# A fused attention kernel: score matmuls over 32 rows in four row groups, a corrected scheduling table and a third buffer set

## The chip, the cores and the metric

The kernel runs on one core of one Trainium2 chip. The metric is device time in microseconds (us), the median of several executions; less is better. In the profile, PE is the matmul engine, PEld its weight loads, ACT the engine that computes exponentials (ScalarE), DVE the vector engine. The granted clock is the share of its full speed that PE's throttle allowed. PSUM is the memory that matmuls write. All runs quoted are fast unless the text says otherwise.

## The reference, cut to what matters

Four blocks on `x` of 2048 tokens and 512 features: multi-query softmax attention (32 heads of 16, one K and one V for all heads), a linear-attention block, and the same two again.

```python
q = (x @ wq).reshape(B, S, 32, 16) ...     # 32 heads
k = x @ wk; v = x @ wv                     # one head of 16 for all
scores = einsum("bhqd,bkd->bhqk", q, k) * 16 ** -0.5
o = einsum("bhqk,bkd->bhqd", softmax(scores), v) ...   # then @ wo
# block B: phi(q) (phi(k)^T v) / den, then @ wo          (linear attention)
```

The two softmax blocks have 2 * 32 * 2048 * 2048 scores. The kernel cuts them into 4096 tiles of 128x512.

## The kernel before: the parts that matter

**Scores.** A head has only 16 features. Q of eight heads lies in 128 partitions, and K is stored in masked copies: in copy `m`, each group of `RG` partitions keeps only the rows of its m-th head, the others are zero. A score matmul contracts one group of `RG` rows against one copy. With `RG = 64` there are two row groups and four copies. Matmuls in different row groups can run at the same time (the timelines below show it).

```python
RG = 64
NRG, NM = P // RG, RG // DH            # 2 row groups, 4 masked copies
i, m = j % NRG, b * (4 // NRG) + j // NRG
r = slice(i * RG, (i + 1) * RG)
x = e.matmul(bank(b0 + k), lhsT=Kr[r, m, kt*P:(kt+1)*P],
             rhs=QT[r, ...], start=True, stop=True)
```

**Two ways to an exponential.** PSUM has eight banks of 128x512. Banks 0 to 2 and 3 to 5 are two *sets*: PE fills one set with three score tiles while ACT turns the other into bf16 exponentials with one instruction (128x1536, "wide"). In parallel, single tiles go through bank 6 to DVE, which approximates the exponential in seven steps, the first on each tile, the other six on pairs of tiles. Bank 7 accumulates the product with V. Whatever else needs a bank (projections, transposes) takes bank 6, or borrows bank 5 (`SHARE`); while that one is lent, ACT gets two tiles only (128x1024, "narrow").

**The order is made at build time.** A small list scheduler simulates the engines with a table of durations and writes a fixed order for each engine. No engine chooses another order at run time:

```python
def tdv(n, c=1.04): return 0.065 + n * c * 1e-3      # DVE, us
def tac(n):         return 0.09 + n * 0.833e-3       # ACT, us
o = add(PE, 0.05 + 0.14 * m, f, ..., name="sA")      # a set of m scores
```

**The filler.** So that PE's clock stays up, the scheduler adds dummy matmuls (zero weights, 512 columns, into the accumulator) wherever PE is idle in its plan and the array streamed less than 0.6 of the last 1.7 us:

```python
st = {"pv": 0.071, "sA": 0.4, "dummy": 0.2}.get(o.name, 0.85 * o.dur[PE])
...                                   # summed over the last 1.7 us
if streaming(now) > FILL * FILLW: return      # FILL, FILLW = 0.6, 1.7
o = add(PE, ..., lambda e: e.matmul(bank(7, FILLN), lhsT=zer[:], ...), name="dummy")
```

The softmax here doesn't subtract the row's maximum and nothing guards it: scores larger than these inputs give would overflow.

## Time and profile before

Median 1849.07 us (1846.9 to 1851.51, 3 runs).

From the page of the kernel before: the span, busy time by engine, the granted clock in 40 slices (9 is 90% or more), and the chain of work that ended last, by engine and by line.

```profile
span 1845.4 us, 26741 instructions
...
PE 1754.5 (95%) x11002; PEld 515.1 (28%) x11002; DVE 1658.7 (90%) x2966; ACT 1739.9 (94%) x1529; POOL 34.2 (2%) x46
...
PEclk9999999999999999999999999999999999999999
...
PE 44%; DVE 43%; ACT 11%; issue 1%; POOL 1%; DMA 0%; SPq 0%
PE ps_all L635 17%; PE ps_all L671 13%; ACT PTA L775 10%; DVE xT L829 9%; DVE PTD L851 8%; PE ps_all L496 7%; DVE xs L850 5%; DVE xs L847 5%; DVE xu L846 4%; DVE xu L849 3%; DVE xs L848 2%; PE ps_all L897 2%; PE ps_all L692 1%; DVE Eo L683 1%; DVE stats L461 1%
...
```

All three engines look nearly full, and the chain changes engine all the time. Neither says what a faster PE is worth. The groups of instructions by shape say more (count, busy us, mean ns of one, then the idle time before them and what ended it):

```profile
...
L775 ACT ACTIVATE PTA<-ps_all 128x1536 bf16<-128x1536 f32 x1039 | 1437.1, 1478 | 57.6 <-PE ps_all L635 50.7
L635 PE MATMUL ps_all<-QT,Kr 64*128 64x512 bf16 x4096 | 835.1, 383 | 42.0 <-DVE xT L829 16.0 <-ACT PTA L775 13.3 <-DVE Osb L701 1.1
...
L829 DVE TENSOR_SCALAR xT<-ps_all 128x512 int32<-128x512 f32 x523 | 358.8, 686 | 48.9 <-PE ps_all L635 45.7
...
L775 ACT ACTIVATE PTA<-ps_all 128x1024 bf16<-128x1024 f32 x227 | 235.5, 1038 | 1.7 <-PE ps_all L635 1.4
L897 PE MATMUL ps_all<-maskx,zer 128*128 128x512 bf16 x594 | 205.0, 387 | 0.0
...
L511 DVE TENSOR_SCALAR Kr<-ps_all,mpar 128x256 bf16<-128x256 f32 x45 | 21.5, 480 | 3.2 <-PE ps_all L496 1.5 <-ACT Kr L510 1.4
...
L510 ACT ACTIVATE Kr<-ps_all,mpar 128x256 bf16<-128x256 f32 x19 | 9.0, 473 | 2.1 <-DVE Kr L511 1.5
...
```

L775 are the exponentials on ACT, wide and narrow; L635 the score matmuls; L829 the first DVE step of a score tile, so 523 of 4096 tiles go to DVE; L897 the dummies; L511 and L510 the evictions of K into its masked copies, 45 + 19 = 64.

A shown duration contains waiting and overlap with the next instruction. The interval from one start to the next is a better price. Where ACT is saturated, a wide exponential starts 1.330 us after the one before it and a narrow one takes 0.903 us. I use that for a balance: **ACT's need** is, for each shape, its count times the 10th percentile of its start-to-start interval; **lateness** is how much longer the intervals after exponentials are in all. For the kernel before, the need is 1698 us, the lateness 47 us after wide and 61 us after narrow exponentials, and 39 us of the span of 1845 us remain (layer starts and ends, mostly).

The timeline of PE (start, length, instruction, how many in a row):

```profile
...
500.62 0.39 PE L635 MATMUL ps_all<-QT,Kr 64*128 64x512 bf16 x2
...
1099.92 0.60 PE L635 MATMUL ps_all<-QT,Kr 64*128 64x512 bf16 x3
...
1104.42 0.82 PE L635 MATMUL ps_all<-QT,Kr 64*128 64x512 bf16 x4
...
```

Two score matmuls in different row groups take as long as one; each time that a row group is needed again, another 0.21 us is added (0.60 and 0.82 us). Who waited for score matmuls (total us, times, longest):

```profile
...
ACT PTA L775 <- PE ps_all L635: 52.1, 127, 1.5
DVE xT L829 <- PE ps_all L635: 45.7, 88, 1.5
...
```

### The profile page before, as it was taken

How to read it: one execution, taken by the hardware profiler on the slowest of the kernel's cores; microseconds unless marked ns; L12 is line 12 of the kernel's file. 1: busy time of each engine (PE TensorE's matmuls, PEld its weight loads, DVE VectorE, ACT ScalarE, POOL GpSimd, SP SyncE). 2: the span in 40 equal slices, each digit the busy share in tenths (PEclk: the TensorE clock that was granted, in tenths of full speed). 3: DMA queues.
4: the chain of work that ended last, by engine and by line, in shares of the span. 5: the costliest groups of instructions: out<-in, count | busy, mean ns of one | idle time of the engine just before them, and what ended most of it. 6: DMA issues, size and time to landing. Idle time of an engine off the chain costs nothing.

```text
span 1845.4 us, 26741 instructions
## 1 busy us (share of the span) xinstructions
PE 1754.5 (95%) x11002; PEld 515.1 (28%) x11002; DVE 1658.7 (90%) x2966; ACT 1739.9 (94%) x1529; POOL 34.2 (2%) x46
## 2 busy tenths in 40 slices
PE   7999999999999999999899999999999999999998
PEld 3222222222222222223342222222223222232224
DVE  7999988999889997998689999899997999989985
ACT  7999999999999999999699999999999999999996
POOL 0000000000000000000000000000000000000000
PEclk9999999999999999999999999999999999999999
DMA  3000000000000000000000000000000000000001
GB/s 115 1 1 1 1 1 1 1 1 1 1 1 1 1 1 1 1 1 1 1 1 1 1 1 1 1 1 1 1 1 1 1 1 1 1 1 1 1 1 46
DMA packets 7722, 9.08 MB, mean 5 GB/s; under 512 B 1456, under 2 KB 7088, under 8 KB 7600
## 3 DMA queue, kind: packets, MB, share of 16 engines
q1 hardware_dynamic: 7600, 7.37, 1.2%
q8 instruction: 86, 1.41, 0.3%
q14 instruction: 36, 0.29, 0.1%
HBM read 5.28 MB, written 2.10 MB: 4 GB/s over the span
## 4 chain that ended last, share of the span: by engine, by line
PE 44%; DVE 43%; ACT 11%; issue 1%; POOL 1%; DMA 0%; SPq 0%
PE ps_all L635 17%; PE ps_all L671 13%; ACT PTA L775 10%; DVE xT L829 9%; DVE PTD L851 8%; PE ps_all L496 7%; DVE xs L850 5%; DVE xs L847 5%; DVE xu L846 4%; DVE xu L849 3%; DVE xs L848 2%; PE ps_all L897 2%; PE ps_all L692 1%; DVE Eo L683 1%; DVE stats L461 1%
## 5 line engine op out<-in xcount | busy, mean ns | idle before, releaser
L775 ACT ACTIVATE PTA<-ps_all 128x1536 bf16<-128x1536 f32 (+1 forms) x1268 | 1640.6, 1398 | 59.4 <-PE ps_all L635 52.1
L635 PE MATMUL ps_all<-QT,Kr 64*128 64x512 bf16 x4096 | 835.1, 383 | 42.0 <-DVE xT L829 16.0
L671 PE MATMUL ps_all<-PTA,Vaug 128*32 128x512 bf16 x3573 | 539.3, 389 | 3.4 <-DVE Eo L683 2.8
L829 DVE TENSOR_SCALAR xT<-ps_all 128x512 int32<-128x512 f32 x523 | 358.8, 686 | 48.9 <-PE ps_all L635 45.7
L851 DVE SCALAR_TENSOR_TENSOR PTD<-xT,xs 128x1024 uint16<-128x1024 int32 (+1 forms) x262 | 318.4, 1215 | 1.4
L635 PEld LDWEIGHTS ps_all<-QT,Kr 64*128 64x128 bf16 x4096 | 175.2, 93 | 500.9 <-ACT PTA L775 198.2
L671 PEld LDWEIGHTS ps_all<-PTA,Vaug 128*32 128x32 bf16 x3573 | 129.5, 93 | 463.4 <-issue 451.5
L897 PE MATMUL ps_all<-maskx,zer 128*128 128x512 bf16 x594 | 205.0, 387 | 0.0
L846 DVE TENSOR_SCALAR xu<-xT 128x1024 f16<-128x1024 uint16 (+1 forms) x262 | 180.2, 688 | 3.0
L850 DVE TENSOR_TENSOR xs<-xs,xu 128x1024 f16<-128x1024 f16 (+1 forms) x262 | 179.0, 684 | 3.0
L847 DVE TENSOR_TENSOR xs<-xu 128x1024 f16<-128x1024 f16 (+1 forms) x262 | 178.7, 682 | 2.0
L671 PE MATMUL ps_all<-PTD,Vaug 128*32 128x512 bf16 x523 | 144.3, 385 | 16.4 <-DVE Eo L683 12.9
L848 DVE TENSOR_SCALAR xs<-xs 128x1024 f16<-128x1024 f16 (+1 forms) x262 | 109.6, 418 | 2.1
L849 DVE TENSOR_SCALAR xu<-xu 128x1024 f16<-128x1024 f16 (+1 forms) x262 | 109.5, 418 | 0.0
L897 PEld LDWEIGHTS ps_all<-maskx,zer 128*128 128x128 bf16 x594 | 48.7, 96 | 105.0 <-issue 98.3
L496 PE MATMUL ps_all<-wqkv_sb,xnT 128*128 128x512 bf16 x256 | 70.9, 383 | 3.3 <-DVE xnT L485 1.1
L469 POOL TENSOR_TENSOR rstd<-veps,mhalf 128x1 f32<-128x1 f32 x30 | 30.7, 1025 | 1731.1 <-DVE veps L467 1723.3
L940 DVE TENSOR_SCALAR e_buf<-e_buf 128x512 f32<-128x512 f32 x64 | 26.9, 422 | 32.8 <-ACT e_buf L939 32.5
L671 PEld LDWEIGHTS ps_all<-PTD,Vaug 128*32 128x32 bf16 x523 | 32.3, 94 | 65.3 <-DVE Eo L683 27.7
L692 PE MATMUL ps_all<-identf,Eo 128*128 128x128 f32 x256 | 42.0, 287 | 5.6 <-DVE Eo L683 4.0
L939 ACT ACTIVATE e_buf<-ps_all 128x512 f32<-128x512 f32 x64 | 39.0, 610 | 8.3 <-PE ps_all L496 6.1
L461 DVE BATCH_NORM_STATS2 stats<-x_sb 128x6 f32<-128x512 bf16 x64 | 43.2, 683 | 3.3 <-DMA x_sb<-in_A_x_dram 2.6
(87 smaller groups left out, 841.6 us busy)
## 6 DMA issues: line engine op xcount, KB each, us to landing
out_dram<-x_sb SPq DMA_DIRECT2D x16, 128.0 KB, 1.7
x_sb<-in_A_x_dram SPq DMA_DIRECT2D x3, 512.0 KB, 6.7
wqkv_sb<-in_B_wqkv_dram SPq DMA_DIRECT2D x1, 1536.0 KB, 11.6
x_sb<-in_A_x_dram SPq DMA_DIRECT2D x2, 256.0 KB, 3.1
wq_sb<-in_A_wq_dram SPq DMA_DIRECT2D x1, 512.0 KB, 4.6
wo_sb<-in_A_wo_dram SPq DMA_DIRECT2D x1, 512.0 KB, 8.5
wo_sb<-in_B_wo_dram SPq DMA_DIRECT2D x1, 512.0 KB, 10.9
wk_sb<-in_A_wk_dram SPq DMA_DIRECT2D x1, 16.0 KB, 2.6
```

What stands on the lines that cost most here:

```text
L496: i = e.matmul(bank(h.idx, n), lhsT=l, rhs=r, start=(c + k == 0), stop=(c + k == len(mms) - 1))
L635: x = e.matmul(bank(b0 + k), lhsT=Kr[r, m, kt * P:(kt + 1) * P], rhs=QT[r, self.units[u][0] % 2, gs, q0:q0 + n], start=True, stop=True)
L671: return e.matmul(ps[32 * c:32 * c + 32, 7 * 512:8 * 512], lhsT=Vaug[:, kt, :], rhs=src, start=opened[0], stop=opened[1], skip_group_check ...
L775: oe = add(AC, tac(m * 512), lambda e: e.activation(PTA[:, hp.idx, 0:m * 512], bank(3 * s, m * 512), ACTF.Exp, scale=SCALE), deps=[o] + pr ...
L829: o = add(DV, tdv(512), lambda e: e.tensor_scalar(out=xT[:, hx.idx, i * 512:(i + 1) * 512], in0=bank(6), scalar1=SCALE * LOG2E * 65536.0, ...
L846: o = add(DV, tdv(w, 0.52), lambda e: e.tensor_scalar(out=u_, in0=lo, scalar1=1.0 / 65536, scalar2=-0.5, op0=ALU.mult, op1=ALU.add), deps= ...
L847: o1 = add(DV, tdv(w, 0.52), lambda e: e.tensor_tensor(out=s_, in0=u_, in1=u_, op=ALU.mult), deps=[o] + c["prev"], name="xsq", **kw)
L848: o2 = add(DV, tdv(w, 0.26), lambda e: e.tensor_scalar(out=s_, in0=s_, scalar1=XK, scalar2=-XW, op0=ALU.mult, op1=ALU.add), deps=[o1], nam ...
L849: o3 = add(DV, tdv(w, 0.26), lambda e: e.tensor_scalar(out=u_, in0=u_, scalar1=1.0, scalar2=XL, op0=ALU.mult, op1=ALU.add), deps=[o1], nam ...
L850: o4 = add(DV, tdv(w, 0.52), lambda e: e.tensor_tensor(out=s_, in0=s_, in1=u_, op=ALU.mult), deps=[o2, o3], name="xc", **kw)
L851: o5 = add(DV, tdv(w), lambda e: e.scalar_tensor_tensor(out=PTD[:, hp.idx, 0:w].bitcast(U16), in0=xT[:, k, 0:w], scalar=2.0 ** -9, in1=s_, ...
L897: o = add(PE, 0.03 + FILLN * 0.41e-3, lambda e: e.matmul(bank(7, FILLN), lhsT=zer[:], rhs=maskx[:].bitcast(BF16)[:, 0:FILLN], start=not ow ...
```

## The change

Scores are to contract 32 rows, so that a set of three uses three of four row groups at once. Two masked copies of K instead of four halve the evictions of K and free the memory for a third set of DVE buffers. The scheduler's table is corrected.

```diff
-    RG = 64
+    RG = 32                      # 4 row groups, 2 masked copies of K
-    NPA, NPD, NDX = 5, 6, 2
+    NPA, NPD, NDX = 5, 6, 3      # sets of DVE buffers
     def tdv(n, c=1.04):
-        return 0.065 + n * c * 1e-3
+        return 0.068 + n * c * 1e-3
     def tac(n):
-        return 0.09 + n * 0.833e-3
+        return 0.0525 + n * 0.8325e-3
... (seven smaller entries, nearly all DVE's: 0.18 -> 0.09, 0.14 -> 0.062, 0.4 -> 0.333 ...)
-            o = add(PE, 0.05 + 0.14 * m, f, ..., name="sA")
+            o = add(PE, 0.2 + 0.014 * m if RG == 32 else 0.05 + 0.14 * m, f, ..., name="sA")
-            st = {"pv": 0.071, "sA": 0.4, "dummy": 0.2}.get(...)
+            st = {"pv": 0.071, "sA": 0.2 if RG == 32 else 0.4, "dummy": 0.2}.get(...)
```

More of the change, by code (lines that the diff above doesn't have):

```diff
@@ L461, in layer_norm @@
         add(DV, tdv(512), lambda e: e.bn_stats(stats[:, t, 0:6], x_sb[:, t, :]), reads=[("x", t)], writes=[("st", t)], prio=prio, name="bn")
-        add(DV, 0.18, lambda e: e.bn_aggr(mv[:, t, :], stats[:, t, 0:6]), reads=[("st", t)], writes=[("mv", t)], prio=prio - 0.01)
+        add(DV, 0.09, lambda e: e.bn_aggr(mv[:, t, :], stats[:, t, 0:6]), reads=[("st", t)], writes=[("mv", t)], prio=prio - 0.01)
         if ctl.ramp or ctl.tail:
@@ L466, in layer_norm @@
         else:
-            add(DV, 0.14, lambda e: e.tensor_scalar(out=veps[:, t:t + 1], in0=mv[:, t, 1:2], scalar1=1e-5, scalar2=None, op0=ALU.add),
+            add(DV, 0.062, lambda e: e.tensor_scalar(out=veps[:, t:t + 1], in0=mv[:, t, 1:2], scalar1=1e-5, scalar2=None, op0=ALU.add),
                 reads=[("mv", t)], writes=[("ve", t)], prio=prio - 0.02)
@@ L485, in cp @@
             return f(xnT[:, :, t * P:(t + 1) * P], bank_bf(hb.idx))
-        o2 = add((DV, AC), {DV: 0.4, AC: tac(512)}, cp, deps=[o], uses=[hb], rel=[hb] + ([win] if win else []), writes=[("xnT", t)], prio=prio - 0.04, name="xnT", cb=cb)
+        o2 = add((DV, AC), {DV: 0.333, AC: tac(512)}, cp, deps=[o], uses=[hb], rel=[hb] + ([win] if win else []), writes=[("xnT", t)], prio=prio - 0.04, name="xnT", cb=cb)
     def proj(h, mms, n, reads, prio, chunk=2, name="proj"):
@@ L513, in k_proj @@
                 ops = {}
-            ops[m] = add((DV, AC), {DV: tdv(b - a), AC: tac(b - a)}, ev, deps=[o] + ([ops[m - 1]] if m else []), uses=[h], rel=[h] if m == NM - 1 else [],
+            ops[m] = add((DV, AC), {DV: 0.06 + tdv(b - a), AC: 0.1 + tac(b - a)}, ev, deps=[o] + ([ops[m - 1]] if m else []), uses=[h], rel=[h] if m == NM - 1 else [],
                          reads=["mpar"], writes=[("K", m, t) for t in range(t0, t0 + n)], prio=prio - 0.05, name="kev")
@@ L694, in norm @@
             o = add(PE, 1.0, tr, reads=["identf"], deps=[oe], acq=[ht, hos] if par == 0 else [ht], uses=[he], rel=[he], prio=1.2, name="trA")
-            o = add(DV, 0.246, lambda e: e.reciprocal(rden[:, hr.idx, :].unsqueeze(2), bank(ht.idx).rearrange("p (a c) -> p a c", c=32)[:, :, DH:DH + 1]),
+            o = add(DV, 0.168, lambda e: e.reciprocal(rden[:, hr.idx, :].unsqueeze(2), bank(ht.idx).rearrange("p (a c) -> p a c", c=32)[:, :, DH:DH + 1]),
                     deps=[o], acq=[hr], uses=[ht], prio=0.0, name="recA")
@@ L769, in f @@
                 return self.smm(e, got, 3 * s)
-            o = add(PE, 0.05 + 0.14 * m, f, reads=self.keys(got), deps=prev, uses=[h], prio=0.0, name="sA")
+            o = add(PE, 0.2 + 0.014 * m if RG == 32 else 0.05 + 0.14 * m, f, reads=self.keys(got), deps=prev, uses=[h], prio=0.0, name="sA")
             hp = Holder(p_pta)
@@ L881, in streaming @@
                 break
-            st = {"pv": 0.071, "sA": 0.4, "dummy": 0.2}.get(o.name, 0.85 * o.dur[PE])
+            st = {"pv": 0.071, "sA": 0.2 if RG == 32 else 0.4, "dummy": 0.2}.get(o.name, 0.85 * o.dur[PE])
             end = o.t0 + o.dur[PE]
@@ L921, in cp @@
             return fn(OT[:, :, g, :] if fine else OT[:, g, :, :], bank_bf(h.idx))
-        o2 = add((DV, AC), {DV: 0.4, AC: tac(512)}, cp, deps=[o], uses=[h], rel=[h], writes=keys, prio=pr, name="otc")
+        o2 = add((DV, AC), {DV: 0.333, AC: tac(512)}, cp, deps=[o], uses=[h], rel=[h], writes=keys, prio=pr, name="otc")
         if fine:
@@ L1021, in kv_block @@
                 for g in (2 * hh, 2 * hh + 1):
-                    add(DV, tdv(P, 0.52), lambda e, g=g: e.tensor_scalar(out=zb[:, g, :], in0=maskx[:, 0:P], scalar1=zf[:, g:g + 1], scalar2=None, op0=ALU.mult),
+                    add(DV, 0.195, lambda e, g=g: e.tensor_scalar(out=zb[:, g, :], in0=maskx[:, 0:P], scalar1=zf[:, g:g + 1], scalar2=None, op0=ALU.mult),
                         reads=[("zf", hh), "mask"], writes=[("zb", g)], prio=0.75, name="zb")
```

## The prediction

> **What bounds the kernel now.** No engine is full, but ScalarE's exponentials set the pace. The busy table gives PE 95%, ACT 94%, DVE 90% of 1845 us. PE's figure is not load (modelled ends, pipelined). ACT's contains hidden waiting: a saturated 128x1536 exponential starts 1.33 us after the one before it (median, timeline), yet is shown 1.48 us long. By such starts, 1039 wide (1.33) and 227 narrow (128x1024, 0.90) exponentials need 1382 + 205 us, and all of ACT about 1690. So some 155 us of ACT are lost: 105 us idle (52 us for score matmuls, waits view), the rest inside durations. The narrow ones, where the third bank is lent, start 1.17 us apart in the mean and lose about 60 us; the wide ones about 47. DVE (523 score tiles) needs about 1600 us and waits 46 us for score matmuls.
>
> **What the change does.**
> - Scores. In the timeline two score matmuls take 0.39 us, three 0.60, four 0.82: a set of three needs two array passes. With four row groups three start together: 0.40 us. That frees about 0.21 us for 1039 sets, 220 us of PE. The Trainium skill ("TensorE: Matmul & The Clock Gate", Part 3) gives 3.07x for four 32-row tiles; this trace shows two 64-row tiles overlapping, not yet four.
> - During a narrow exponential (0.90 us) PE must refill the other set: about 0.4 us of signalling and order plus 0.60 of matmuls does not fit; with 0.40 it just does. I expect 35 of the 60 us back, and 15 of the 47.
> - K: 64 evictions become 32; DVE loses about 10 us of work, ACT 4.5 us, at layer starts; perhaps 6 us of span.
> - Scheduling table: it decides a static order. The old one charged 1.369 us for a wide exponential, the new one 1.331, what the trace shows. The old one paced ACT 3% too slow and gave DVE too many tiles; perhaps 10 us. A third DVE buffer set covers some of DVE's waits.
> - Against it: the filler that keeps the clock up sees half the streaming per set and adds dummies (0.22 us each); from 594 I expect about 1300. They eat much of the freed PE time, but enter only where the schedule has PE idle. Narrow exponentials stay near 230.
>
> "TensorEngine Tiling (Array Packing)", PSUM Bottleneck, says that tiling speeds up TensorE but not PSUM evacuation; that is why only waiting, not ACT or DVE work, is won here: about a quarter of the 220 us.
>
> **Sum.** 35 + 15 + 6 + 10, less some lost to dummies and to DVE not keeping up: about 50 us. Predicted 1798 us, 8 in 10 between 1755 and 1838. Faster by over 2% (below 1812): 0.64; within 2%: 0.32; slower: 0.04.
>
> **What would show it.** Three score matmuls in 0.40 us; narrow exponentials about 1.0 us apart in the mean; ACT's waits for scores below 30 us; ACT busy about 96%; dummies over 1000; 32 K evictions; granted clock 1.00 throughout; DVE tiles 500 to 540.
>
> **What would make it wrong.** Row groups that don't run together; the filler delaying score sets as before; a lower clock; the lent bank, not matmul time, stalling narrow sets (then about 1835); ACT waiting for the order of PE's queue behind DVE-released work, which faster scores don't cure; DVE taking over as the limit. If the corrected table matters more than I think, below 1760.

## The result and the profile after

Median 1799.83 us (1795.13 to 1806.72, 4 runs) against 1849.94 us (4 runs) before: ratio 0.9734, 95% interval 0.9692 to 0.9776. All ratios here are the mean time of one kernel's fast runs over that of the other's fast runs of the same rounds, so not quite the ratio of the medians.

The same parts of the page, for the kernel after:

```profile
span 1804.9 us, 27782 instructions
...
PE 1730.1 (96%) x11478; PEld 542.5 (30%) x11478; DVE 1671.0 (93%) x3022; ACT 1719.8 (95%) x1552; POOL 27.2 (2%) x46
...
PEclk9999999999999999999999999998999999999999
...
PE 46%; ACT 32%; DVE 21%; issue 1%; DMA 0%; SPq 0%
ACT PTA L775 31%; PE ps_all L635 14%; PE ps_all L671 14%; PE ps_all L496 7%; PE ps_all L897 6%; DVE xT L829 4%; DVE PTD L851 4%; DVE xs L847 2%; DVE xs L850 2%; DVE xu L846 2%; DVE xu L849 1%; DVE xs L848 1%; PE ps_all L1060 1%; DVE stats L461 1%; DVE Eo L683 1%
...
```

The chain holds more ACT (32% against 11%) and less DVE (21% against 43%). One slice of the clock row has fallen to 8. The clock differs between runs: two had a mean clock of 0.999 and took 1795 us, two had 0.991 and 0.993 and took 1807 and 1804 us. The groups:

```profile
...
L775 ACT ACTIVATE PTA<-ps_all 128x1536 bf16<-128x1536 f32 x943 | 1328.6, 1516 | 37.4 <-PE ps_all L635 34.1
L635 PE MATMUL ps_all<-QT,Kr 32*128 32x512 bf16 x4096 | 662.7, 386 | 35.2 <-ACT PTA L775 16.3 <-DVE xT L829 6.7 <-DVE Osb L701 3.0
...
L775 ACT ACTIVATE PTA<-ps_all 128x1024 bf16<-128x1024 f32 x362 | 390.6, 1079 | 2.1 <-PE ps_all L635 1.1
L829 DVE TENSOR_SCALAR xT<-ps_all 128x512 int32<-128x512 f32 x542 | 370.5, 684 | 48.0 <-PE ps_all L635 44.8
L897 PE MATMUL ps_all<-maskx,zer 128*128 128x512 bf16 x1070 | 363.1, 389 | 0.0
...
L511 DVE TENSOR_SCALAR Kr<-ps_all,mpar 128x256 bf16<-128x256 f32 x26 | 12.3, 475 | 0.3
...
L510 ACT ACTIVATE Kr<-ps_all,mpar 128x256 bf16<-128x256 f32 x6 | 2.8, 475 | 1.5 <-PE ps_all L496 0.9 <-DVE Kr L511 0.4
...
```

Three score matmuls now run in the time of one, and so do four in four different groups (the first line; it happens 27 times in this trace). Where a fourth meets a used row group, it waits (the last line):

```profile
...
72.42 0.40 PE L635 MATMUL ps_all<-QT,Kr 32*128 32x512 bf16 x4
...
1040.42 0.39 PE L635 MATMUL ps_all<-QT,Kr 32*128 32x512 bf16 x3
...
1045.70 0.61 PE L635 MATMUL ps_all<-QT,Kr 32*128 32x512 bf16 x4
...
```

The waits:

```profile
...
DVE xT L829 <- PE ps_all L635: 44.8, 78, 1.8
ACT PTA L775 <- PE ps_all L635: 35.2, 90, 1.7
...
```

Narrow exponentials rose from 227 to 362, dummies from 594 to 1070, DVE tiles from 523 to 542; K evictions fell to 32 (26 on DVE and six on ACT). The balance closes:

| profiled run | span | ACT's need | late after wide | late after narrow | rest |
|---|---|---|---|---|---|
| before | 1845 | 1698 | 47 | 61 | 39 |
| after | 1805 | 1686 | 33 | 46 | 40 |

Of 40 us, 29 are lateness and 12 are work that left ACT. The latter I can account for: 19 more tiles on DVE at 0.443 us are 8 us, 13 fewer K evictions on ACT at 0.37 us are 5 us, and the extra narrow exponentials cost 135 * 2 * 0.009 = 2 us. In the profiled runs of all later kernels but one (slow) the rest is 36 to 42 us, so **need and lateness account for the span.** (That ACT's intervals add up to the span is so by construction; what is found is that the rest hardly changes. Why an exponential is late, the balance doesn't say.)

Since the order is fixed at build time, each exponential can be paired in the trace with its own score matmuls. A *refill* then has two parts: the **order delay**, from the end of the last work that held the set's banks to the first score matmul, and the **fill**. Medians in us:

| profiled run | order delay, beside a wide exponential | beside a narrow one | fill | dummies |
|---|---|---|---|---|
| before | 0.34 | 0.40 | 0.60 | 594 |
| after | 0.39 | 0.25 | 0.39 | 1070 |

("Beside": the exponential that runs just before the set's own, while it is refilled.) The fill is 0.21 us shorter, as expected. Before, 0.40 + 0.60 us do not fit into a narrow exponential's 0.90 us; after, 0.25 + 0.39 us do in the median. Nearly all late exponentials, after as before, belong to sets with an order delay: PE was still at other work. In front of late sets in the kernel before stood 63 us of projections, 68 us of products with V and 29 us of dummies; after, 43, 45 and 45 us.

### The profile page after: what moved, and what is told of

It is laid out like the page before. It is cut to its first block, busy times and chain, and to the rows that moved or that the text cites. A ratio compares the mean times of both kernels' runs of the same rounds, so it can differ in the third digit from the quotient of the medians.

```text
span 1804.9 us, 27782 instructions
## 1 busy us (share of the span) xinstructions
PE 1730.1 (96%) x11478; PEld 542.5 (30%) x11478; DVE 1671.0 (93%) x3022; ACT 1719.8 (95%) x1552; POOL 27.2 (2%) x46
## 4 chain that ended last, share of the span: by engine, by line
PE 46%; ACT 32%; DVE 21%; issue 1%; DMA 0%; SPq 0%
ACT PTA L775 31%; PE ps_all L635 14%; PE ps_all L671 14%; PE ps_all L496 7%; PE ps_all L897 6%; DVE xT L829 4%; DVE PTD L851 4%; DVE xs L847 2%; DVE xs L850 2%; DVE xu L846 2%; DVE xu L849 1%; DVE xs L848 1%; PE ps_all L1060 1%; DVE stats L461 1%; DVE Eo L683 1%
## 5 line engine op out<-in xcount | busy, mean ns | idle before, releaser
L635 PE MATMUL ps_all<-QT,Kr 32*128 32x512 bf16 x4096 | 662.7, 386 | 35.2 <-ACT PTA L775 16.3
L897 PE MATMUL ps_all<-maskx,zer 128*128 128x512 bf16 x1070 | 363.1, 389 | 0.0
L851 DVE SCALAR_TENSOR_TENSOR PTD<-xT,xs 128x1024 uint16<-128x1024 int32 x271 | 328.6, 1213 | 0.4
L635 PEld LDWEIGHTS ps_all<-QT,Kr 32*128 32x128 bf16 x4096 | 158.8, 91 | 509.3 <-ACT PTA L775 220.8
L846 DVE TENSOR_SCALAR xu<-xT 128x1024 f16<-128x1024 uint16 x271 | 184.8, 682 | 1.1
L850 DVE TENSOR_TENSOR xs<-xs,xu 128x1024 f16<-128x1024 f16 x271 | 184.0, 680 | 0.7
L847 DVE TENSOR_TENSOR xs<-xu 128x1024 f16<-128x1024 f16 x271 | 184.0, 679 | 0.7
L848 DVE TENSOR_SCALAR xs<-xs 128x1024 f16<-128x1024 f16 x271 | 112.2, 414 | 0.3
L849 DVE TENSOR_SCALAR xu<-xu 128x1024 f16<-128x1024 f16 x271 | 112.1, 414 | 0.0
L683 DVE COPY Eo<-ps_all 128x512 f32<-128x512 f32 x63 | 43.1, 684 | 5.6 <-PE ps_all L671 5.2
```

The lines of the kernel that those rows point to most:

```text
L635: x = e.matmul(bank(b0 + k), lhsT=Kr[r, m, kt * P:(kt + 1) * P], rhs=QT[r, self.units[u][0] % 2, gs, q0:q0 + n], start=True, stop=True)
L846: o = add(DV, tdv(w, 0.52), lambda e: e.tensor_scalar(out=u_, in0=lo, scalar1=1.0 / 65536, scalar2=-0.5, op0=ALU.mult, op1=ALU.add), deps= ...
L847: o1 = add(DV, tdv(w, 0.52), lambda e: e.tensor_tensor(out=s_, in0=u_, in1=u_, op=ALU.mult), deps=[o] + c["prev"], name="xsq", **kw)
L848: o2 = add(DV, tdv(w, 0.26), lambda e: e.tensor_scalar(out=s_, in0=s_, scalar1=XK, scalar2=-XW, op0=ALU.mult, op1=ALU.add), deps=[o1], nam ...
L849: o3 = add(DV, tdv(w, 0.26), lambda e: e.tensor_scalar(out=u_, in0=u_, scalar1=1.0, scalar2=XL, op0=ALU.mult, op1=ALU.add), deps=[o1], nam ...
L850: o4 = add(DV, tdv(w, 0.52), lambda e: e.tensor_tensor(out=s_, in0=s_, in1=u_, op=ALU.mult), deps=[o2, o3], name="xc", **kw)
```

## The experiments

My theory (A): the time is won because a set is refilled sooner. Rivals: (B) the new order, made with the corrected table, wins it; (C) the K evictions and the third buffer set do. Kernels ran beside the kernel before (medians 1848.3, 1849.3 and 1850.1 us).

### The order of before, scores in four row groups

The order of instructions is the same on every engine; the result is wrong.

```diff
-                r = slice(i * RG, (i + 1) * RG)
+                r = slice(j * 32, (j + 1) * 32)
```

> The kernel before, with every instruction in the same order on every engine; only each score matmul reads 32 rows, in the row group of its own head of four, so that a set of three fits in one array pass. The result is wrong on purpose. Theory A (the time is won because a set is refilled 0.2 us sooner): most of the gain is here already, about 1810 to 1825 us, and narrow exponentials start about 1.05 us apart instead of 1.17. Rival B (the time is won by the new order of instructions that the corrected scheduling table makes): no gain, 1840 to 1850 us. Rival C (K evictions and third DVE buffer): no gain either, 1845 to 1850 us.

Measured: 1900.14 us, ratio 1.0268, slower, which none of the theories expected. From its page:

```profile
span 1902.6 us, 26741 instructions
...
PEclk9998999877989999899998978997589977899999
...
```

The mean clock is 0.905; the kernel before, in the same rounds, had 0.998 to 1.000. The records hold 362 us at half clock, in stretches that are multiples of 3.41 us. The Trainium skill ("TensorE: Matmul & The Clock Gate", Part 1) states a half-rate state and a window of 3413 ns; this trace agrees with both. Nothing but the row groups was changed, and the clock fell in all four runs (0.905 to 0.914): with faster scores the 594 dummies that were planned for slow ones no longer hold it. That the reason is an array that streams less (some 0.2 us less per set of three) is argued, not shown.

The run still speaks for A. With equal orders, stretches of ten ACT instructions can be compared one by one. The 96 stretches with no half clock in or just before them took 1073.8 us before and 1043.5 us here: 2.8% less, with nothing changed but the row groups. It isn't catching up after a slow stretch: the 41 stretches with no half clock in the 50 us before them took 446.5 us before and 434.0 us here, 2.8% less again. So at full clock faster scores win time by themselves, without a new order, fewer K evictions or a third buffer set.

### The order of after, scores in two row groups

Same order as after, but a set of three takes two passes again; wrong result.

```diff
-                r = slice(i * RG, (i + 1) * RG)
+                r = slice(i % 2 * RG, (i % 2 + 1) * RG)
```

> The kernel after, with every instruction in the same order on every engine; only the score matmuls are put in two of the four row groups, so that a set of three needs two passes again, as before. The result is wrong on purpose. Theory A: the gain is lost, 1835 to 1860 us, because the static order now counts on refills that come late. Rival B: the order keeps most of its gain, 1800 to 1815 us. Rival C: as B, about 1800 to 1810 us.

Measured: ratio 1.0624; two fast runs at 1964 us with clock 0.978, two slow ones at 2072 and 2145 us. All three ranges are missed. The lower clock is not the whole of it: in the kernel after, a mean clock lower by 0.007 went with 10 us, so 0.021 would be some 30 us (an estimate), of more than 110. So the new order does not stand on its own: it counts on fast sets. B, as I had stated it, falls. (The profiled run is a slow one. Its paired stretches without half clock took 1526 us against 1419 us, which fits, but the argument rests on the fast runs.) From the page of that slow run:

```profile
...
PE   8999999999999999999999999999999999999999
...
PEclk9999999999999999659985555575589999999999
...
```

PE is at 90% or more in the busy row in all slices but the first, and yet stayed at half clock for 276 us on end (the slices of 5). Since only a slow run shows this stretch, it may belong to the slow state and not to the row groups; nothing is built on it. Why the clock did not recover stays open.

### The table alone

```diff
 (kernel after)
-    RG = 32
+    RG = 64
-    NPA, NPD, NDX = 5, 6, 3
+    NPA, NPD, NDX = 5, 6, 2
```

(With 64 rows three DVE buffer sets do not fit in on-chip memory: the build stops with 752 bytes of a partition left and 2064 wanted. The third set is there only because two copies of K are gone.)

> Corrected scheduling table alone: 64 rows, four copies of K, two DVE buffer sets. Theory A: little, 1835 to 1850 us (the prediction put the table at 10 us). Rival B: most of the 50 us, 1800 to 1815 us. Rival C: nothing, 1849 us.

Measured: 1829.85 us, ratio 0.9898, so 18.5 us less than before, at a clock of 0.998 to 1.000. It lies between the ranges of A and B: all three miss. The gain is almost twice what I gave the table.

### 32 rows alone

```diff
 (kernel before)
-    RG = 64
+    RG = 32
-            o = add(PE, 0.05 + 0.14 * m, f, ..., name="sA")
+            o = add(PE, 0.2 + 0.014 * m, f, ..., name="sA")
-            st = {"pv": 0.071, "sA": 0.4, "dummy": 0.2}...
+            st = {"pv": 0.071, "sA": 0.2, "dummy": 0.2}...
```

> 32 rows, two copies of K, and the entries of the scheduling table that follow from that (a set of three costs 0.24 us, streams 0.2 us); all other entries old, two DVE buffer sets. Theory A: most of the gain, 1805 to 1820 us. Rival B: little, 1835 to 1850 us. Rival C: the K part alone, 1840 us.

Measured: 1829.44 us, ratio 0.99, so 18.9 us less. Theory A expected 1805 to 1820 and misses, and so do the other two. The 18.9 us hold the halved K evictions too; no run parts them from the faster scores. The refills show where the rest went: the fill fell from 0.60 to 0.39 us, but the order delay rose from 0.34 to 0.54 us beside wide exponentials and from 0.40 to 0.57 us beside narrow ones. Most of what the matmuls won per set, the wait in PE's queue took back. There are 1270 dummies, and in front of late sets their share rose from 29 to 66 us.

### 32 rows and the table, without the third buffer set

```diff
 (kernel after)
-    NPA, NPD, NDX = 5, 6, 3
+    NPA, NPD, NDX = 5, 6, 2
```

> The kernel after with two DVE buffer sets instead of three: 32 rows and the corrected table together. If the parts simply add (table alone gave 18.5 us, 32 rows alone 18.9 us of 1848.3), 1811 us, and the third buffer set is worth the remaining 11 us. If the parts need one another, about 1800 us and the third set is worth nothing. If the third set is what unlocks the gain, about 1825 us.

Measured: 1812.59 us, ratio 0.9801. That is where the two parts would be if they simply add (1811 us). The third buffer set is then worth 0.9801 - 0.9734, or 12 us, but a part of this is the clock: all four runs here had 0.989 to 0.992. At a like clock, the two runs at 0.991 and 0.992 took 1810 and 1811 us, and the two of the kernel after at 0.991 and 0.993 took 1807 and 1804 us: some 5 us.

### 32 rows and the third buffer set, with the old table

```diff
 (32 rows alone)
-    NPA, NPD, NDX = 5, 6, 2
+    NPA, NPD, NDX = 5, 6, 3
```

> The kernel after with the old table: 32 rows and three DVE buffer sets. If parts add, about 1800 + 18.5 = 1818 us. If the third set only pays with the corrected table, 1829 us like 32 rows alone. The third set should cut DVE's wait for score matmuls, 55 us with 32 rows alone, to below 50 us.

Measured: 1846.39 us, ratio 0.9981. Both expectations miss: with the old table the third set *costs* 15 us (0.9981 against 0.99), about half of it clock: at a clock of 0.995 this kernel took 1841 us and 32 rows alone 1833 us (one run each). DVE's wait for scores did fall, from 55 to 49 us. The chain and the first DVE step:

```profile
...
DVE 52%; PE 41%; ACT 4%; issue 3%; DMA 0%; SPq 0%; POOL 0%
PE ps_all L635 13%; PE ps_all L671 12%; DVE xT L829 12%; DVE PTD L851 10%; PE ps_all L496 7%; PE ps_all L897 6%; DVE xu L846 5%; DVE xs L850 5%; DVE xs L847 5%; ACT PTA L775 3%; DVE xu L849 3%; DVE xs L848 3%; DVE Eo L683 2%; DVE stats L461 1%; PE ps_all L1060 1%
...
```

```profile
...
L829 DVE TENSOR_SCALAR xT<-ps_all 128x512 int32<-128x512 f32 x562 | 385.2, 685 | 51.5 <-PE ps_all L635 48.7
...
```

DVE takes 562 tiles and holds 52% of the chain, ACT 4%; the order delay beside wide exponentials is 0.58 us and the lateness 128 us.

### The third set, the old table, and one corrected entry

To find the entry that did this, only ACT's is corrected:

```diff
 (old table, 32 rows, three buffer sets)
     def tac(n):
-        return 0.09 + n * 0.833e-3
+        return 0.0525 + n * 0.8325e-3
```

> The kernel after with the old table except for the one entry of ACT (a wide exponential charged 1.331 us instead of 1.369); DVE's entries old. With the whole old table the same kernel took 1846 us, with the whole new one 1800. Theory P (the old ACT entry paces the shared PE queue 3% too slow and hands DVE too many tiles, 562 instead of 542): this one entry brings nearly all back, 1797 to 1810 us, with 539 DVE tiles. Rival Q (DVE's small entries, several of them 0.07 to 0.09 us too long, matter as much): 1815 to 1835 us.

Measured: 1798.81 us, ratio 0.9725, in P's range and as fast as the whole change; 539 DVE tiles. One entry, 0.038 us per exponential, is worth 2.6% of the run here (48 us, 44 us at a like clock of 0.990 to 0.992), and the DVE entries nothing that shows. DVE's share of the chain falls from 52% to 26%:

```profile
...
PE 40%; ACT 31%; DVE 26%; issue 2%; DMA 0%; POOL 0%; SPq 0%
...
```

How the entry works is not shown. It is tempting that 0.038 us on some 1280 exponentials are 49 us, as if an ACT planned 3% too slow were made to run 3% too slow. But the same sum would give the two comparisons with two buffer sets 49 us too, and there the whole table brought 18 us each (1 to 0.9898, 0.99 to 0.9801). Nor is ACT slowed evenly with the old entry: half of the wide exponentials still start within 1.331 us of the one before. What the runs show is a better order with fewer DVE tiles and 54 us less lateness (128 to 74).

### Fast sets planned as slow ones

32 rows, old table, two buffer sets, and the old cost of a set; the filler knows the true streaming.

```diff
 (32 rows alone)
-            o = add(PE, 0.2 + 0.014 * m ..., name="sA")
+            o = add(PE, 0.05 + 0.14 * m, f, ..., name="sA")
```

> 32 rows alone, but the schedule is built with the old cost of a set (0.47 us for three) while the filler knows the true streaming of 0.2 us, so there are 978 dummies instead of 594. The result is right. Theory A (the set's physical 0.2 us is what pays; the clock drop, not the order, spoilt the run of the old order with four row groups, where stretches at full clock were 2.8% shorter): 1800 to 1830 us with a clock of 0.99 or more. Rival B (the order must be made for the fast sets): 1840 us or more at a full clock.

Measured: 1826.19 us (1821 to 1845), ratio 0.9909, clock 0.969 to 0.987. Within A's range, with a lower clock than A asked for; not different from 32 rows alone (0.99). The true cost of a set in the plan is thus worth nothing that this run shows; fast sets, with the halved K evictions that come with them, are. It has 292 dummies fewer than 32 rows alone and a lower clock; the two may cancel.

### A higher threshold for the filler

```diff
 (kernel after)
-    FILL, FILLW, FILLN = 0.6, 1.7, 512
+    FILL, FILLW, FILLN = 0.7, 1.7, 512
```

> The kernel after with the filler's threshold at 0.7 instead of 0.6: 1532 dummies instead of 1070. The clock should stay at 1.00 in all runs (the kernel after had 0.991 to 0.999; 1795 us at 0.999, 1805 at 0.992). If dummies delay sets: 1800 to 1815 us in spite of the better clock. If they do no harm: 1793 to 1796 us.

Measured: 1844.46 us, ratio 0.9972, with a clock of 1.00 in all four runs: worse than any theory expected. The chain, and the dummies:

```profile
...
PE 76%; DVE 15%; ACT 6%; issue 2%; DMA 0%; SPq 0%; POOL 0%; ACTq 0%
PE ps_all L635 25%; PE ps_all L671 23%; PE ps_all L897 17%; PE ps_all L496 7%; ACT PTA L775 4%; DVE xT L829 3%; DVE PTD L851 2%; DVE Eo L683 2%; DVE xs L850 1%; DVE xu L846 1%; DVE xs L847 1%; PE ps_all L692 1%; PE ps_all L1060 1%; DVE stats L461 1%; PE ps_all L1000 1%
...
```

```profile
...
L897 PE MATMUL ps_all<-maskx,zer 128*128 128x512 bf16 x1366 | 438.6, 385 | 12.8 <-issue 12.7
...
L897 PEld LDWEIGHTS ps_all<-maskx,zer 128*128 128x128 bf16 x1532 | 113.0, 97 | 242.2 <-issue 218.6
...
```

(Some records of matmuls are missing from this trace; the 1532 weight loads give the count.) PE holds 76% of the chain, dummies alone 17%. The order delay beside wide exponentials rose from 0.39 to 0.66 us and the lateness from 79 to 113 us. Against the runs after at a clock of 0.999, 462 more dummies cost 49 us. **So a filler that adds more than the clock needs costs time,** and dummies in the queue in front of the sets are my account of where much of the faster scores' gain goes. That account is argued: each of these kernels has a new order on every engine, and the next run does not bear it out.

### Shorter dummies

```diff
 (kernel after)
-    FILL, FILLW, FILLN = 0.6, 1.7, 512
+    FILL, FILLW, FILLN = 0.6, 1.7, 256
-            st = {..., "dummy": 0.2}...
+            st = {..., "dummy": 0.1}...
```

> The kernel after with dummies of 256 columns instead of 512, 1974 of them instead of 1070, about the same array time but half the delay of each. In the trace of the kernel after, dummies are the largest piece of work (45 us) that stands in PE's queue between a bank's release and a late set's first matmul. If that is lost to dummies, a dummy of half the length delays a set half as much: 1780 to 1793 us. If the dummies only fill time in which the set would have waited for other work anyway: 1795 to 1805 us. If short dummies keep the clock up less well: above 1805 us with a clock below 0.99.

Measured: 1826.71 us, ratio 0.9869, clock 0.984 to 0.995. The first two ranges are missed: 1974 short dummies stand in front of late sets for 48 us, not less than 1070 long ones, and the lateness is 102 us instead of 79. The third, a lower clock, holds only in part: the run with the best clock, 0.995, still took 1818 us, and the kernel after took 1804 us at 0.993. What else makes it slower stays open.

### No lending

```diff
 (kernel after)
-    SHARE = True
+    SHARE = False
```

> The kernel after, but the sixth score bank is never lent: 3 narrow exponentials instead of 362, 1204 wide, 478 DVE tiles instead of 542. A narrow exponential costs 0.452 us per tile against 0.443, so ACT saves only 362*0.018 = 6.5 us on the same tiles but takes 64 more tiles of 0.443 us = 28 us. If ACT's work sets the pace: 1815 to 1830 us, slower. If what the lent bank stalls (46 us after narrow exponentials) sets it: 1770 to 1785 us, faster, unless other work waiting for the one free bank gives it back.

Measured: 1781.11 us, ratio 0.9633 (0.9611 to 0.9655): in the second range, and the best. Chain and groups:

```profile
...
ACT 60%; DVE 21%; PE 18%; issue 1%; DMA 0%; POOL 0%; SPq 0%
ACT PTA L775 57%; PE ps_all L635 5%; PE ps_all L671 5%; DVE xT L829 4%; DVE PTD L851 3%; PE ps_all L897 3%; PE ps_all L496 2%; DVE xu L846 2%; DVE xs L847 2%; DVE xs L850 2%; ACT e_buf L939 1%; DVE stats L461 1%; DVE xs L848 1%; DVE xu L849 1%; PE ps_all L1060 1%
...
```

```profile
...
L775 ACT ACTIVATE PTA<-ps_all 128x1536 bf16<-128x1536 f32 x1204 | 1640.8, 1571 | 6.5 <-PE ps_all L635 5.1
...
L829 DVE TENSOR_SCALAR xT<-ps_all 128x512 int32<-128x512 f32 x478 | 328.2, 687 | 79.0 <-PE ps_all L635 76.9
...
```

ACT holds 60% of the chain. Its need is higher, 1706 us, and its lateness 32 us instead of 79: after wide exponentials it stayed (31 us, 33 before), after narrow ones it is gone with them. Whether the lent bank stalled those sets, or a narrow exponential is too short to refill behind, this run doesn't part. ACT's wait for scores fell from 35 us to 5; DVE's rose from 45 to 77, and yet DVE's share of the chain is 21% as in the kernel after.

### No lending and short dummies

```diff
 (short dummies, above)
-    SHARE = True
+    SHARE = False
```

> The kernel after without lending a bank and with short dummies (2214): the candidate for the best. Not lending alone gave 1781 us (0.9633 of before), with 28 us of late exponentials left, 26 us of dummies in front of the late ones. If short dummies halve their share: 1765 to 1775 us. If not: 1776 to 1785 us.

Measured: 1787.73 us, ratio 0.9664. A little slower than no lending alone, and outside both ranges, at a lower clock (0.990 to 0.998 against 0.994 to 1.000).

### All kernels in one table

| profiled run | ratio of times | span | ACT's need | lateness | rest | dummies | DVE tiles |
|---|---|---|---|---|---|---|---|
| before | 1 | 1845 | 1698 | 108 | 39 | 594 | 523 |
| table alone | 0.9898 | 1827 | 1702 | 85 | 40 | 553 | 514 |
| 32 rows alone | 0.99 | 1828 | 1690 | 101 | 36 | 1270 | 531 |
| both | 0.9801 | 1809 | 1697 | 77 | 36 | 1162 | 516 |
| 32 rows, third set, old table | 0.9981 | 1845 | 1678 | 128 | 39 | 1216 | 562 |
| the same, ACT's entry corrected | 0.9725 | 1802 | 1685 | 74 | 42 | 1154 | 539 |
| after (all three) | 0.9734 | 1805 | 1686 | 79 | 40 | 1070 | 542 |
| after, more dummies | 0.9972 | 1843 | 1688 | 113 | 42 | 1532 | 538 |
| after, no lending | 0.9633 | 1778 | 1706 | 32 | 40 | 1234 | 478 |

## Why the prediction was right, and where it was not

The time was 2 us from the forecast, but the split behind it was only partly right, and that the sum came so close is luck. Forecast were 56 us for faster scores and K evictions, 10 for the table, nothing for the third buffer set. Measured one after another they are 19, 18 and 12 us.

- **What bounds the kernel: right.** ACT's work plus waiting that hides inside its durations. Need and lateness account for every fast run.
- **Three scores in the time of one: right** (0.39 us; 0.60 before). The Trainium skill ("TensorE: Matmul & The Clock Gate", Part 3) gives 3.07x for four tiles; here three in 0.39 us against 0.39 for one agree with its picture, and so do the 27 cases of four different groups (0.39 to 0.40 us for all four). The figure 3.07 itself no run here shows.
- **35 + 15 us of lateness: over-sized at the narrow end.** Measured 15 after narrow and 14 after wide exponentials. Per narrow exponential the lateness did halve (61/227 = 0.27 to 46/362 = 0.13 us), but there were 362 and not "near 230". And this is not the scores' gain alone: 32 rows alone won 19 us in all, with the K evictions, though at full clock in the old order faster scores took 2.8% off. I had the filler's harm as "some lost"; by the order delay in front of the sets and the run with more dummies it seems larger; how large was not measured.
- **The table, "perhaps 10 us": too small.** 18.5 us alone, and 47 us in the presence of the third buffer set. The named entry, ACT's, was the right one where it was tested alone, with three buffer sets; the named way, the pace, is not shown.
- **The third buffer set:** named, not costed. It is worth 12 us with the corrected table and minus 15 with the old one; at a like clock some 5, and minus 8.
- **K evictions: right in count** (32), 5 us of ACT's work. What they are worth in the span was not tested alone.
- **Smaller signs.** Narrow exponentials 1.03 us apart in the mean, after 1.17 (said: about 1.0). ACT busy 95% (said: about 96); its waits for scores 35 us (said: below 30); DVE tiles 542 (said: 500 to 540); dummies 1070 (said: about 1300). The granted clock was said to stay at 1.00; it was 0.991 to 0.999, and the runs with 0.99 took about 10 us longer.
- **The quoted limit of evacuation** (the skill's "TensorEngine Tiling (Array Packing)", PSUM Bottleneck) agrees with the trace: a wide exponential started 1.33 us after the one before it both times, and ACT's need stayed within 1%. Of the 40 us, 29 are waiting; most of the rest is work that left ACT, not work that got faster.
- The lent bank was listed as a risk ("then about 1835"). Taking the lending away gave another 1%, and the 46 us of lateness after narrow exponentials went with them.

So the sum hit because an over-sized term (faster scores) and two under-sized ones (the table, the buffer set) happened to cancel. What stays open: how much of the 2.8% seen at full clock the scores would bring if dummies cost nothing, how one entry of the table comes to be worth so much, what the K evictions are worth, and why the clock fell with two row groups.

## What to carry to other kernels

In a statically ordered kernel a faster step pays only if the in-order queue lets its consumer start sooner: measure the delay from "bank free" to "first matmul" apart from the length of the matmuls, and look at what fills the freed time. Price durations in the scheduler by start-to-start intervals of saturated stretches; with three buffer sets an error of 3% on the pacing engine cost 2.6% here, and with it the extra buffer was a loss; with two sets the whole table was worth 1%. Compare kernels at a like clock before crediting a change of 1%. When matmuls get shorter, re-check what keeps the clock up before judging the idea: with the old filler the same fast matmuls lost 2.7%.

## What the Trainium skill lacked or had wrong

- "TensorE: Matmul & The Clock Gate", Part 1, says that the clock depends on how busy PE has been; it does not say how row-tiled matmuls count. The order of before with four row groups had PE busy for 90% of the span in the profile, and a mean clock of 0.905 to 0.914 in four fast runs; with scores over 64 rows in the same order it had 0.998 to 1.000.
- The same page's rule ("Why this matters for your kernels": no idle gaps above some 3 us between bursts) is not enough here: the order of before with four row groups had no idle gap of PE above 1.3 us after its start, and spent 362 us at half clock (mean clock 0.905). Part 1 of the page does tell of short, frequent idles that make the clock swing ("A second HAM failure mode"), but gives no measure of how many are too many.
- "TensorEngine Tiling (Array Packing)" names the pressure on PSUM that row tiling brings, but not that a packed kernel may need filler matmuls for its clock: with 594 it fell to 0.905, with 1070, in the new order, it was 0.991 to 0.999, and with 462 more 1.00, at 1844 us instead of 1795.
- "ScalarE: Activation LUTs", What ACT_TABLE_LOAD costs, gives 186 ns + 0.833 ns per element for an activation with immediate operands and an overlap of about 93 ns back to back. For 1536 elements that is 1.373 us, an estimate from that page and nearly the old table's 1.369. The saturated interval here is 1.330 us, and 0.904 us for 1024 elements: about 50 ns + 0.833 ns per element. The old table's entry was close to the page's figure; bringing it to the measured one was worth 48 us with three buffer sets.
